# Gated-H3 forward and backward on one core: which engine transposes the gate gradient of three tiles, and how the FFT stage is ordered

## The chip, the core and the metric

The kernel runs on one core of a Trainium2 chip. A core has TensorE (PE, matrix products, whose weight loads the profile shows apart as PEld), VectorE (DVE), ScalarE (ACT), GpSimd (POOL) and SyncE (SP), and 16 DMA engines. The metric is the device time in microseconds (us) of one execution.

## The reference

What is computed is a block with a long convolution and a gated linear unit, forward and then backward by `jax.vjp`. S = 2048 positions, D = 512 channels, F = 1376 hidden columns.

```python
xn = layernorm(q)
k_shift = sum_t k_pad[:, t:t+S, :] * shift_k[:, 3-t]     # 4 taps
kv = k_shift * v
y  = irfft(rfft(kv, 2S) * rfft(ssm_k, 2S))[:, :S] + kv * ssm_D
s  = xn * y
h  = sigmoid(xn @ w_gate) * (xn @ w_up)
out = q + s * silu(h @ w_down)
# and the gradients of q, k, v, shift_k, ssm_k, ssm_D, w_gate, w_up, w_down for a given grad_out
```

The outputs are `out` and the nine gradients. The FFT is done as products with cosine and sine tables on TensorE.

## The kernel before

The program is not issued as it is written. A recorder, class Rec, takes down every operation with what it reads and writes (`add`); at the end `order()` makes one static order for each engine, and `emit()` issues it. So every instruction stands at line 522 in the profile, and the order of the code decides only between operations that the planner holds ready at the same time. `order()` simulates: each operation has an estimated duration (`cost`, `dcost`), each engine a time at which it is free, and in each step the operation that can start first is taken, of several the one that was recorded first.

- **Either engine.** An evacuation of PSUM (`evac`, line 238) may go to ScalarE or VectorE. VectorE takes it if ScalarE would come too late for it by more than 0.4 us, or 1.6 us where VectorE has other work waiting (lines 420 to 426). `op.bias` (0.3 us for PSUM of 2-byte type, which is what transposes leave there) is taken off VectorE's start in this comparison.
- **Dependent neighbours.** From operation `late` to operation `early`, an operation on VectorE or ScalarE that reads what the same engine wrote is taken as ready 0.034 us after the other's end (line 507, `r = fin + 0.034`), and an independent one may be taken in between, with a look-ahead of 0.125 us (`near`). Outside this stretch the successor counts as ready when the engine is free. Before, `late` is set at the end of the FFT stage (line 1076), `early` at the end of stage B.

The work has three stages.

**FFT stage** (operations 0 to 2405, up to about 130 us). Four streams are interleaved by `run_streams`: strG, the forward products of the gated unit (`f_gen`) for nine tiles of 128 positions in the order 15, 13, 11, 9, 7, 5, 0, 1, 2; strK, the transform of the convolution's kernel in four channel groups (`k_t` transposes the input, `step1` is the first product, `flip` transposes on TensorE, `step3` the second product); strV, shifted k times v (four taps on VectorE, each on 128x2048 elements, multiply and add, then `step1`); strX, `flip` and `step3` of kv, the products of the spectra on VectorE, and back (`inv3`, `inv1`). `gen_ci` transposes the tables. It begins with `gen_fft_consts`, which makes the tables on VectorE and ScalarE (Sin), and with the loads: `ld_KT`, `ld_k` (k and, on the same queue, its halo of three rows), `ld_v`, `ld_x`, `ld_w` (columns of both weights), all on SP's queue; skr (shift_k) and Dcol_b (ssm_D) on ScalarE's queue. `k_t(0)` adds Dcol_b to the first column before it transposes. Four products with a row of ones spread skr over the partitions (skb), which strV reads.

**Stage B** (`stepB`), tile by tile 0 to 15: `z_gen` (the down projection and the gradient of the gate, dz), `d_gen` (gradient through w_down, which needs dz transposed, dzT), `x_gen` (gradient of the input) and the rest of the `f_gen` tiles. dzT of tile 0 and of tiles 13 to 15 is made by four TensorE transposes and an evacuation, that of tiles 1 to 12 by one DMA transpose on SP's queue (line 1155).

**Last stage**: gradients of the weights (`dW`) and the backward convolution (`frontC`, `backC`).

SBUF is one tile that an arena divides (all its parts are called slab in the profile), PSUM likewise (psum).

Of the kernel before, what the change touches and what calls it, by code (L numbers as in the profile page):

```python
# [16 lines left out]
P = 128  # L17
# [6 lines left out]
NJ = 16  # L24
# [128 lines left out]
def esize(dt):  # L153
    return 4 if dt in (f32, i32) else 2


class Op:
    __slots__ = ("n", "alts", "deps", "succ", "wait", "ready", "dma", "tiles", "done", "fin", "eng", "soft", "bias")


class EngRec:
# [9 lines left out]
class Rec:  # L171
# [8 lines left out]
    def __init__(self, nc, tc, slab, psum):  # L180
        self.nc, self.tc, self.psum = nc, tc, psum
        self.slab_name = slab.name
        self.ops = []
        self.lastw, self.readers = {}, {}
        self.late, self.early = 1 << 30, 1 << 30
        self.cache = {}
        for e in self.ENGS:
            setattr(self, e, EngRec(self, e))
# [47 lines left out]
        return r  # L236

    def evac(self, dst, src, n):
        op = self.add([("scalar", "copy", (dst, src), {}), ("vector", "tensor_copy", (dst, src), {})])
        op.bias = 0.3 if esize(src.ap.dtype) == 2 else 0  # L240

    def add(self, alts):
        op = Op()
# [106 lines left out]
    def order(self):  # L350
# [55 lines left out]
        while ndone < len(ops):  # L406
            best = None
            for e in self.ENGS:
                near = 0.125 if e in ("vector", "scalar") and self.late <= lo < self.early else 0.0
                while soon[e] and soon[e][0][0] <= free[e] + near:  # L410
                    heapq.heappush(now[e], heapq.heappop(soon[e])[1])
                c = None
                if now[e]:
                    n0 = now[e][0]
                    if near and ops[n0].ready > free[e]:
                        n0 = min((n for n in now[e] if ops[n].ready <= free[e] and n < n0 + 60), default=n0)
                    c = (max(free[e], ops[n0].ready) if near else free[e], n0, e, 0)
                elif soon[e]:
                    c = (soon[e][0][0], soon[e][0][1], e, 0)
                if either and e in ("scalar", "vector"):  # L420
                    o = min(either, key=lambda o: (max(o.ready, free[e]) - (o.bias if e == "vector" else 0.0), o.n))
                    s = (max(o.ready, free[e]), o.n, e, 1)
                    late = free["scalar"] - s[0] + o.bias
                    if e == "scalar" or late > (0.4 if c is None or c[0] > s[0] + 0.6 else 1.6):
                        if c is None or s[:2] < c[:2]:
                            c = s
                if c is not None and (best is None or c[:2] < best[:2]):
                    best = c
            if best is None:
                raise RuntimeError("the order is stuck: " + str({k: len(v) for k, v in blocked.items()}))  # L430
            t, n, e, shared = best
            op = ops[n]
            if shared:
                either.remove(op)
            else:
                if now[e]:
                    now[e].remove(n)
                    heapq.heapify(now[e])
                else:
                    heapq.heappop(soon[e])  # L440
            q = 1 if shared and e == "vector" else 0
            new = [v for v in op.tiles if v.bank is None]
            if new:
                got = slot(new[0].kind)
                if got is None:
                    blocked[new[0].kind].append(op)
                    continue
                if got[0] > t:
                    op.ready = got[0]
                    push(op)  # L450
                    continue
                new[0].bank = got[1][0]
                for b in got[1]:
                    owner[b] = new[0]
            alt = op.alts[q]
            d = 0.0
            if op.dma:
                occ, d = self.dcost(alt)
                me, other = ("gpsimd", "hw") if e == "gpsimd" else ("hw", "gpsimd")
                t = max(t, pipe[me] - 12.0)  # L460
                t0 = max(pipe[me], t + 1.5)
                share = min(d, max(0.0, pipe[other] - t0))
                pipe[me] = t0 + d + share
                if share:
                    pipe[other] += share
                fin = pipe[me] + (DSL if t > 6 else 1.0)
            else:
                occ, lat = self.cost(alt)
                if e == "scalar" and alt[1] == "activation":
                    f = {ACT.Sin: "sin", ACT.Sigmoid: "sig"}.get(alt[2][2])  # L470
                    if f and f != table:
                        table = f
                        occ, lat = occ + 1.28, lat + 1.28
                fin = t + lat
            free[e] = t + occ
            op.done, op.fin, op.eng = True, fin, e
            seq.append((op, q, t, occ, d))
            ndone += 1
            while lo < len(ops) and ops[lo].done:
                lo += 1  # L480
            while held and held[0] <= lo + LOOK:
                o = ops[heapq.heappop(held)]
                o.ready = max(o.ready, t)
                push(o)
            for v in op.tiles:
                v.left -= 1
                v.last = max(v.last, fin)
                if v.left == 0:
                    for b in range(8):
                        if owner[b] is v:  # L490
                            owner[b] = None
                            banks[b] = v.last + 0.05 + PSL
                    for kind, lst in blocked.items():
                        for o in lst:
                            o.ready = max(o.ready, 0.0)
                            push(o)
                        lst.clear()
            for s in op.succ:
                if s < 0:
                    o = ops[~s]  # L500
                    o.wait -= 1
                    if o.wait == 0:
                        push(o)
                    continue
                o = ops[s]
                if e == o.alts[0][0] and len(o.alts) == 1 and not op.dma:
                    r = fin + 0.034 if e in ("vector", "scalar") and self.late <= o.n < self.early else t + occ
                else:
                    r = fin + 0.045 + (PSL if o.alts[0][0] == "tensor" and not op.dma else 0.0)
                o.ready = max(o.ready, r)  # L510
                o.wait -= 1
                if o.wait == 0:
                    push(o)
# [123 lines left out]
def kernel_impl(ctx, tc, A_q, A_k, A_v, A_shift_k, A_ssm_k, A_ssm_D, B_x, B_w_gate, B_w_up, B_w_down,  # L637
# [23 lines left out]
    def ps_acc(shape, dt=f32, name=None):  # L661
        return nc.ps("acc", shape, dt)
# [151 lines left out]
    def ld_v(cp):  # L814
        vg = vg_r.next()
        nc.sync.dma_start(vg, vC[:, :, cp * GW:(cp + 1) * GW])
        stA["vg", cp] = vg
# [4 lines left out]
    def ld_x(i):  # L822
        T[i]["xq"] = xq_r.next()
        nc.sync.dma_start(T[i]["xq"], qC[:, i, :])
    nc.scalar.dma_start(skr, A_shift_k.rearrange("(o d) t -> o (d t)", o=1))
    nc.scalar.dma_start(Dcol_b, A_ssm_D.rearrange("(cg p) -> p cg", p=P))
    ld_KT(0)
    ld_x(SEQ[0])
    ld_x(SEQ[1])
# [1 line left out]
    def ld_w(f0, f1):  # L831
        for w, src in ((wg, B_w_gate), (wu, B_w_up)):
            nc.sync.dma_start(w[:, :, f0:f1], src[:, f0:f1].rearrange("(db p) f -> p db f", p=P))
    ld_w(0, 512)
    ld_k(0)
    ld_v(0)
    ld_x(SEQ[2])
    ld_w(512, 1024)
    ld_w(1024, F)
# [22 lines left out]
        pass  # L862
    next(consts)
    f_ln(SEQ[0])
    next(consts)
    f_xt(SEQ[0])
    f_ln(SEQ[1])
    next(consts)
    for db in range(4):
        pb = ps_acc([512])  # L870
        nc.tensor.matmul(pb[:], ones1, skr[:, db * 512:(db + 1) * 512], start=True, stop=True)
        nc.scalar.copy(skb[:, :, db * 128:(db + 1) * 128], pb[:].rearrange("p (d t) -> p t d", t=4))
    ld_KT(1)
    ld_k(1)
    ld_v(1)
# [197 lines left out]
    for r in (KT_r, KC_r, kh_r, vg_r, acc_r, term_r, kvt_r, QgK_r, QgV_r, QfK_r, QfV_r, KF_r, Ks_r, Bg_r, Xc_r, P1_r, Ci_r):  # L1073
        r.free()
    PS["mm"], PS["wide"] = "mm1", False
    nc.late = len(nc.ops)


    zw = {k: Ring(ar, [D], at=kv_off["kh"] + 1024 * q) for q, k in enumerate(("sigz", "gate", "s_out", "dgate", "t2"))}
# [53 lines left out]
    def z_gen(i):  # L1133
# [18 lines left out]
        nc.vector.tensor_tensor(t2, t2, sigz, ALU.add)  # L1152
        nc.vector.tensor_tensor(dzA[:, i, :], dgate, t2, ALU.mult)
        T[i]["dzT"] = dzT_r.next()
        if 0 < i < NJ - 3:
            nc.sync.dma_start_transpose(T[i]["dzT"], dzA[:, i, :])
        else:
            pt = ps_tr([4, 128], name="ps_dzT")
            for db in range(4):
                nc.tensor.transpose(pt[:, db, :], dzA[:, i, db * 128:(db + 1) * 128], ident)  # L1160
            nc.evac(T[i]["dzT"], pt[:], 512)
# [380 lines left out]
```

## Time and profile before

| what | us |
|---|---|
| median of 13 runs | 519.66 (518.68 to 521.81) |
| the profiled execution | 519.77 |
| its span, first to last instruction | 518.0 |
| busy: TensorE | 491.9 |
| busy: VectorE | 390.5 |
| busy: ScalarE | 351.2 |
| busy: GpSimd | 126.0 |

The page cuts the span in 40 slices, and a digit gives the busy share of an engine in a slice in tenths. A matmul's record runs from its issue to its modelled end, so TensorE's busy time holds waits within a group of products too. The timeline puts successive instructions of one form into one row: start, duration, engine, line, operation, output and input, and how many. In the groups by shape a row gives count, summed busy time, the mean of one in ns and, behind the next bar, the idle time of the engine just before them with what ended it.

The first slices of ScalarE and VectorE:

```profile
DVE  8789998777848789867779988427658678873754
ACT  7799999889975564465545546426879968776621
```

### The profile page before, as it was taken

Reading aid. Unit: us, or ns where it says so; the run is one execution under the profiler, and the core shown is the slowest. Engines: PE = TensorE matmul, PEld = TensorE weight load, DVE = VectorE, ACT = ScalarE, POOL = GpSimd, SP = SyncE. Lnnn points to the kernel's source line nnn. Section 1 sums busy time; section 2 is a strip of 40 time slices with the busy share of each in tenths; the row PEclk is TensorE's granted clock in tenths of the full one; section 3 lists DMA queues with packets and bytes.
Section 4 is the critical chain, followed back from the end, with each engine's and each line's share of the span. In section 5 each row is a group of like instructions: output and inputs, shape, how many; then the busy total and the mean of one; then the engine's idle time right before and its main releaser. Section 6 shows DMA issues by size and latency. Waiting matters only on the chain.

```text
span 518.0 us, 13489 instructions
## 1 busy us (share of the span) xinstructions
PE 491.9 (95%) x5381; PEld 352.7 (68%) x5437; DVE 390.5 (75%) x771; ACT 351.2 (68%) x468; POOL 126.0 (24%) x243
## 2 busy tenths in 40 slices
PE   4899898999999999999999999999999999999997
PEld 3788697898987676666666556644676756775744
DVE  8789998777848789867779988427658678873754
ACT  7799999889975564465545546426879968776621
POOL 7344423455503423414153311000000000000000
PEclk9999998999999999999999999999999999999999
DMA  8999985688999555737399947898798689999984
GB/s 221 295 279 330 296 260 183 208 253 245 235 198 236 156 160 149 221 100 200 117 251 232 267 156 179 208 295 215 180 254 227 189 260 215 259 199 253 200 219 120
DMA packets 181705, 112.93 MB, mean 218 GB/s; under 512 B 131433, under 2 KB 166153, under 8 KB 181386
## 3 DMA queue, kind: packets, MB, share of 16 engines
q1 hardware_dynamic: 170008, 78.17, 62.9%
q0 software_dynamic: 11104, 33.89, 19.9%
q8 instruction: 42, 0.69, 0.5%
q14 instruction: 21, 0.17, 0.1%
q10 hardware_dynamic: 530, 0.01, 0.1%
HBM read 37.65 MB, written 45.72 MB: 161 GB/s over the span
## 4 chain that ended last, share of the span: by engine, by line
PE 74%; ACT 10%; DVE 7%; issue 3%; DMA 3%; POOL 1%; SPq 0%; ACTq 0%; DVEq 0%; POOLq 0%
PE psum L522 74%; ACT slab L522 10%; DVE slab L522 7%; DMA out_dram<-slab 1%; DMA slab<-in_A_ssm_D_dram 1%; POOL slab L522 1%; DMA slab<-in_grad_out_dram 0%; SPq L522 0%; ACTq L522 0%; POOL hF_d L522 0%; POOL out_dram L522 0%; DVEq L522 0%; POOLq L522 0%
## 5 line engine op out<-in xcount | busy, mean ns | idle before, releaser
L522 PE MATMUL psum<-slab 128*128 128x128 bf16 (+5 forms) x5381 | 491.9, 254 | 22.4 <-ACT slab L522 10.3
L522 PEld LDWEIGHTS <-slab 128*128 128x128 bf16 (+2 forms) x5437 | 352.7, 99 | 161.3 <-issue 17.0
L522 DVE TENSOR_TENSOR slab<-slab 128x512 bf16<-128x512 bf16 (+6 forms) x488 | 268.6, 601 | 51.8 <-ACT slab L522 34.2
L522 ACT CAST slab<-psum 128x1024 bf16<-128x1024 f32 (+5 forms) x272 | 219.7, 848 | 93.4 <-PE psum L522 79.7
L522 ACT ACTIVATE slab<-psum 128x512 bf16<-128x512 f32 (+2 forms) x80 | 54.2, 680 | 39.3 <-PE psum L522 36.1
L522 ACT ACTIVATE slab<-slab 128x512 bf16<-128x512 bf16 (+3 forms) x71 | 56.8, 810 | 15.0 <-DVE slab L522 14.1
L522 ACT COPY slab<-psum 128x1024 bf16<-128x1024 bf16 (+1 forms) x43 | 38.4, 939 | 14.1 <-PE psum L522 13.9
L522 POOL DMA_DIRECT2D out_dram<-slab x32 | 17.4, 545 | 95.8 <-DVE slab L522 95.8
L522 DVE TENSOR_TENSOR slab<-psum,slab 128x512 bf16<-128x512 f32 (+2 forms) x47 | 29.3, 627 | 14.1 <-ACT slab L522 12.2
L522 DVE CAST slab<-psum 128x1024 bf16<-128x1024 f32 (+2 forms) x22 | 24.6, 1117 | 15.0 <-PE psum L522 12.9
L522 POOL MEMSET slab<- 1x384 bf16 (+2 forms) x13 | 4.8, 375 | 116.7 <-PE psum L522 116.3
L522 POOL DMA_DIRECT2D hF_d<-slab x48 | 26.0, 544 | 23.3 <-DVE slab L522 22.3
L522 DVE SCALAR_TENSOR_TENSOR slab<-psum,slab 128x512 bf16<-128x512 f32 x16 | 11.0, 690 | 27.1 <-PE psum L522 27.1
L522 POOL DMA_DIRECT2D KK_d<-slab x32 | 17.4, 545 | 27.6 <-ACT slab L522 20.5
L522 POOL DMA_DIRECT2D slab<-in_A_q_dram x29 | 16.0, 554 | 15.3 <-DVE slab L522 4.7
L522 DVE SCALAR_TENSOR_TENSOR slab<-slab 128x512 bf16<-128x512 bf16 (+3 forms) x41 | 17.1, 417 | 0.9
L522 DVE STREAM_TRANSPOSE slab<-slab 128x1024 f32<-128x1024 f32 x8 | 14.3, 1824 | 2.7 <-ACT slab L522 2.7
L522 DVE TENSOR_SCALAR slab<-slab 128x1 f32<-128x1 f32 (+9 forms) x48 | 12.1, 268 | 4.6 <-POOL slab L522 3.7
L522 POOL TENSOR_TENSOR slab<-slab 128x1 f32<-128x1 f32 x16 | 11.2, 700 | 17.5 <-DVE slab L522 17.2
L522 POOL DMA_DIRECT2D slab<-hF_d x18 | 9.7, 541 | 12.7 <-PE psum L522 11.5
L522 DVE BATCH_NORM_STATS2 slab<-slab 128x6 f32<-128x512 bf16 x16 | 10.9, 686 | 0.0
L522 DVE COPY slab<-psum 128x1024 bf16<-128x1024 bf16 (+1 forms) x14 | 9.0, 649 | 2.3 <-ACT slab L522 1.7
(20 smaller groups left out, 36.2 us busy)
## 6 DMA issues: line engine op xcount, KB each, us to landing
KK_d<-slab POOLq DMA_DIRECT2D x32, 256.0 KB, 5.0
slab<-KK_d SPq DMA_DIRECT2D x16, 512.0 KB, 4.5
slab<-in_A_k_dram SPq DMA_DIRECT2D x8, 512.0 KB, 7.8
hF_d<-slab POOLq DMA_DIRECT2D x32, 128.0 KB, 4.6
slab<-slab SPq DMA_DIRECT2D x32, 128.0 KB, 5.2
out_dram<-slab POOLq DMA_DIRECT2D x32, 128.0 KB, 2.9
uF_d<-slab SPq DMA_DIRECT2D x32, 128.0 KB, 2.5
gF_d<-slab SPq DMA_DIRECT2D x32, 128.0 KB, 2.9
```

Source lines behind the costliest of these rows:

```text
L522: getattr(getattr(self.nc, eng), meth)(*[place(v) for v in a], **{x: place(v) for x, v in k.items()})
```

## The change

Four things change together.

1. `evac` sets no bias, and `order()` does not use one.
2. `late` is 0 from the start and not set again, so the rule for dependent neighbours holds in the FFT stage too.
3. The start: Dcol_b is loaded ahead of skr; k and v of group 0 are loaded ahead of the first columns of the weights; the four skb products and their copies are recorded right behind the first layernorm.
4. dzT of tiles 10, 11 and 12 is made by TensorE transposes and an evacuation instead of a DMA transpose.

```diff
-        self.late, self.early = 1 << 30, 1 << 30
+        self.late, self.early = 0, 1 << 30
...
     def evac(self, dst, src, n):
-        op = self.add([("scalar", "copy", (dst, src), {}), ("vector", "tensor_copy", (dst, src), {})])
-        op.bias = 0.3 if esize(src.ap.dtype) == 2 else 0
+        self.add([("scalar", "copy", (dst, src), {}), ("vector", "tensor_copy", (dst, src), {})])
...
-                    o = min(either, key=lambda o: (max(o.ready, free[e]) - (o.bias if e == "vector" else 0.0), o.n))
+                    o = min(either, key=lambda o: (max(o.ready, free[e]), o.n))
                     s = (max(o.ready, free[e]), o.n, e, 1)
-                    late = free["scalar"] - s[0] + o.bias
+                    late = free["scalar"] - s[0]
...
+    nc.scalar.dma_start(Dcol_b, A_ssm_D.rearrange("(cg p) -> p cg", p=P))
     nc.scalar.dma_start(skr, A_shift_k.rearrange("(o d) t -> o (d t)", o=1))
-    nc.scalar.dma_start(Dcol_b, A_ssm_D.rearrange("(cg p) -> p cg", p=P))
...
-    ld_w(0, 512)
     ld_k(0)
     ld_v(0)
+    ld_w(0, 512)
...
     f_ln(SEQ[0])
+    for db in range(4):
+        pb = ps_acc([512])
+        nc.tensor.matmul(pb[:], ones1, skr[:, db * 512:(db + 1) * 512], start=True, stop=True)
+        nc.scalar.copy(skb[:, :, db * 128:(db + 1) * 128], pb[:].rearrange("p (d t) -> p t d", t=4))
     next(consts)
     f_xt(SEQ[0])
     f_ln(SEQ[1])
     next(consts)
-    for db in range(4):
-        pb = ps_acc([512])
-        nc.tensor.matmul(pb[:], ones1, skr[:, db * 512:(db + 1) * 512], start=True, stop=True)
-        nc.scalar.copy(skb[:, :, db * 128:(db + 1) * 128], pb[:].rearrange("p (d t) -> p t d", t=4))
...
-    nc.late = len(nc.ops)
...
-        if 0 < i < NJ - 3:
+        if 0 < i < 10:
             nc.sync.dma_start_transpose(T[i]["dzT"], dzA[:, i, :])
         else:
             pt = ps_tr([4, 128], name="ps_dzT")
             for db in range(4):
                 nc.tensor.transpose(pt[:, db, :], dzA[:, i, db * 128:(db + 1) * 128], ident)
             nc.evac(T[i]["dzT"], pt[:], 512)
```

From about 30% of the program on, the new order of every engine is the old one but for the three tiles of point 4. Before that, 28 evacuations change their engine and many operations their place.

More of the change, by code (lines that the diff above doesn't have):

```diff
@@ L157 @@
 class Op:
-    __slots__ = ("n", "alts", "deps", "succ", "wait", "ready", "dma", "tiles", "done", "fin", "eng", "soft", "bias")
+    __slots__ = ("n", "alts", "deps", "succ", "wait", "ready", "dma", "tiles", "done", "fin", "eng", "soft")
 class EngRec:
```

## Prediction

> **What bounds the kernel now.** The profiled execution has a span of 518.0 us in a time of 519.77; the median of the thirteen runs shown is 519.66, so sums on the trace are read against 519.77 and 0.11 is taken off at the end. About ±1.04 us (0.2%) is what can be told from no change.
>
> I read the page's engine rows first, then its slices, then the windows of the stages.
>
> ```profile
> PE 491.9 (95%) x5381; PEld 352.7 (68%) x5437; DVE 390.5 (75%) x771; ACT 351.2 (68%) x468; POOL 126.0 (24%) x243
> ...
> PE   4899898999999999999999999999999999999997
> ...
> PEclk9999998999999999999999999999999999999999
> ```
>
> TensorE is busy 95% at full clock, but a matmul that waits for its buffer counts as busy too. So I price a step by its pitch in a stream:
>
> ```profile
> 34.70 0.61 PE L522 MATMUL psum<-slab 128*128 128x128 bf16 x8 [0.35 <-ACT slab L522]
> 35.62 0.55 PE L522 MATMUL psum<-slab 128*128 128x128 bf16 x7 [0.31 <-ACT slab L522]
> ```
>
> Eight 128-column steps took 0.61 us. One alone takes 0.22 (their mean in the groups by shape), so one more costs (0.61 - 0.22)/7 = 0.056 us; the second row is transposes against the identity (gen_ci): (0.55 - 0.22)/6 = 0.055, the same. A 512-column step, from 21 in 4.70 us that begin at 275.66, is (4.70 - 0.38)/20 = 0.216.
>
> With these, 20 to 70 us holds 648 x 0.056 + 19 x 0.216 = 40 us of TensorE work in 50; 260 to 300 holds 39.4 in 40. Summed the same way over the span, TensorE loses 28 us before 100 us (14 of them in the first 20, some 9 from 20 to 70, 5 from 80 to 98), nothing worth naming from 100 to 360, and 3 after. **A TensorE instruction added after 100 us costs its full pitch; before 100 us the time is set by who feeds TensorE.** That is read in the windows (time, and busy time of each engine with its instructions, then clock, DMA share, GB/s):
>
> ```profile
> 20.00:70.00 50.00, 44.12 (x667) 39.17 (x670) 45.17 (x61) 46.58 (x58) 21.47 (x40) 1.00 0.99 298
> ...
> 80.00:98.00 18.00, 15.54 (x199) 13.29 (x199) 16.11 (x23) 16.55 (x19) 7.64 (x13) 0.91 0.48 155
> ...
> 104.00:130.00 26.00, 25.57 (x410) 23.71 (x412) 19.29 (x34) 23.52 (x29) 14.41 (x27) 1.00 0.85 249
> ```
>
> From 20 to 70 us VectorE (45.2) and ScalarE (46.6) are both nearly full; from 30 on each is busy over 39 of 40. At 104 to 130 TensorE is full and ScalarE has 26 - 23.5 = 2.5 us to spare.
>
> **Part 1: dzT of tiles 10, 11, 12 on TensorE.** Three DMA transposes leave SP's queue, three evacuations of 128x512 and twelve TensorE steps come. In the trace the transpose of tile 10 was issued at 274.25, landed at 278.62, and d_gen(10) began at 280.2; tiles 11 and 12 took 4.3 and 4.8 us and no product waited for them. So nothing is won by removing them, and the stores behind them on SP gain about 1.2 us of issue each, which nothing waits for. The evacuations (0.60 us each) go to ScalarE, busy 20.8 of the 40 us from 260 to 300; other TensorE work stands between. If that cover failed, d_gen would wait at most one evacuation per tile, 1.8 us in all.
>
> The price of the steps is where a rule speaks against the change. The row: 12 x 0.056 = **+0.67 us**. The Trainium skill ("TensorE: Matmul & The Clock Gate", Part 4, PE-mode transpose) gives about 275 ns for a 128x128 transpose inside a kernel and says that transposes don't count as busy for the clock: by it, an estimate of 12 x 0.275 = 3.3 us. The transposes in this trace run at 0.055 behind each other with the clock at 1.00, so I take the row; 3.3 is the upper end.
>
> **Part 2: no lean by type.** Before, an evacuation of 2-byte PSUM leaned to VectorE by 0.3 us. The new static order has seven more bf16 evacuations of 1024 on ScalarE, and four fewer f32 ones there.
>
> ```profile
> L522 ACT CAST slab<-psum 128x1024 bf16<-128x1024 f32 x150 | 148.8, 1042 | 28.9 <-PE psum L522 19.1 <-DVE slab L522 5.5 <-DMA out_dram<-slab 2.7
> L522 ACT COPY slab<-psum 128x1024 bf16<-128x1024 bf16 x32 | 32.3, 1055 | 4.8 <-PE psum L522 4.6
> ...
> L522 DVE CAST slab<-psum 128x1024 bf16<-128x1024 f32 x18 | 22.0, 1221 | 8.7 <-PE psum L522 6.6 <-DMA out_dram<-slab 2.1
> L522 DVE COPY slab<-psum 128x1024 bf16<-128x1024 bf16 x12 | 8.2, 686 | 1.0 <-PE psum L522 0.6 <-ACT slab L522 0.5
> ```
>
> ScalarE: 7 x 1.06 - 4 x 1.04 = +3.2 us; VectorE: 4 x 1.22 - 7 x 0.69 = +0.1. VectorE takes a bf16 tile 0.37 us cheaper than ScalarE and an f32 tile 0.18 dearer, so the exchange costs work on the pair. By place, from the two orders with these means: up to about 98 us ScalarE has +1.1 and VectorE +0.4; from there to 130 ScalarE gets another 2.8 us.
>
> **Part 3: the order of the FFT stage with the delay of dependent operations.** VectorE has 52 of 201 neighbouring pairs there in which the second reads the first; after, 31 of 197. In the trace a dependent successor starts 0.03 us after the end (84.63 after 84.60), an independent one about 0.08 before it (80.04 in the operation of 79.43 to 80.12): 21 x 0.11 = 2.3 us of VectorE. Of this the sum takes the row; "VectorE: DVE Perf Modes" (The DRAIN you can't avoid) lets no successor start before the pipe is empty, by which reordering would give 0. The same section says that one not held starts earlier, so the row stands.
>
> At 80 to 98 us TensorE starves; the chain of waits goes through VectorE there:
>
> ```profile
> 81.26 3.34 DVE slab L522 x4
> ```
>
> In the timeline VectorE runs five 128x2048 products of strV (1.22 us each, depending on each other) from 80.64 on, with one f_gen product between them, and the product of strX that TensorE needs starts only at 87.03. In the new order one strV product and one small operation fewer stand ahead of it: 1.22 + 0.55 = 1.8 us. ScalarE's queue stands full beside it until 90, so I count the share of VectorE on this chain: (3.34 + 0.69)/18 x 1.8 = -0.4.
>
> **Part 4: the start.** D's load is issued first (0.75 instead of 1.30): it landed at 6.26 and VectorE waited 0.53 for it, so VectorE is up to 0.56 earlier. The four skb broadcasts and their copies move before later Sin operations, same work. k and v of group 0 go ahead of the first 1 MB of weights. SP needed 3.17 to 9.53 us to issue k's two pieces; w_up landed at 9.91, and behind k and v would land near 16, while the first f_gen product began at 14.75. So f_gen(15) is up to 1.5 us later, but k's second halo gets off the queue earlier, and strV(0), which waited until 28.92 for a halo issued at 23.96, starts about 3 us sooner and fills VectorE's 4.2 idle us of 20 to 30.
>
> **Sum.** Up to 104 us: VectorE -2.3 + 0.4 = -1.9, ScalarE +1.1. Both are full and hand work to each other, so half of the sum, -0.4; the stall -0.4; the start I put at 0 (ScalarE's queue reaches the same point at 30 us with one more evacuation done, but the first f_gen later). Together **-0.8**, bounds -2.9 (VectorE alone decides: -2.3 - 0.56 + 0.38 - 0.4) and +1.5 (the weights decide). 104 to 130: +2.8 us on ScalarE against 2.5 spare: 0.4 if all the idle time can be used, 2.8 if none; TensorE needs its buffers in turn, so the middle, **+1.4** after taking 0.2 off for the 1 us that VectorE gives back. Part 1 **+0.7**. In all +1.3: 521.0 in its own execution, 520.9 against the median. Own range: -0.8 + 0.4 + 0.7 = +0.3 at the low end; at the high end the FFT stage loses a third of its upper bound, +0.5, and ScalarE's extra counts whole: +0.5 + 2.8 + 0.7 = +4.0. So 519.9 to 523.7.
>
> **Rivals.**
> A, faster: VectorE is what TensorE waits for all through the FFT stage, so its dependent gaps and the stall at 81 to 88 come off in full: -2.9 + 0.4 + 0.7 = -1.8, **517.9**; with the whole 1.8 of the stall and ScalarE's extra hidden, -3.6, 516.1. For: the chain at 81 us, DVE 39.4 of 40 from 30 to 70. Against: ScalarE 39.6 of 40 there. It decides once strX's product ends more than ScalarE's backlog ahead of 87.
> B, no net change: FFT stage -0.8, ScalarE's extra at 104 hidden, twelve steps +0.7: **519.6**. For: VectorE has 6.7 idle us there. Against: the order is fixed, so idle VectorE takes nothing over.
> C, slower at the start: the weights landing at 16 hold the first f_gen and with it ScalarE's sigmoid: +1.5 instead of -0.8, **523.2**. For: DMA 0.96 busy in the first 20 us. Against: step1 products are there to be done.
>
> **Chances.** Forecast 0.36, A 0.34, B 0.18, C 0.12. Faster takes A and a little of B, 0.35; within 0.2% B and the lower edge of the forecast, 0.20; slower 0.45. The range reaches into A to 516.8 and into C to 523.5.
>
> **What would show it.** Part 1: no idle TensorE at 270 to 300, twelve more steps, clock 1.00. Part 2: ScalarE near 26 of 26 at 104 to 130 and TensorE waiting on it; if TensorE streams there, the +1.4 falls. Part 3: strX's product earlier than 87.03 against f_gen(7), TensorE's loss of 80 to 98 below 5 us; if it is under 3, A holds. Part 4: strV(0) before 27, first f_gen near 16. Wrong altogether if the first 20 us move by over 2 us either way.

## The result, and the profile after

The changed kernel took 524.85 us (median of 11 runs, 522.46 to 527.71), the kernel before 519.59 in the same comparison (48 runs): a ratio of 1.0097, 95% interval 1.0082 to 1.0113. It is slower, as forecast, but by four times as much as the forecast of 520.9 said, and above both upper ends that the prediction names (523.5 and 523.7). The profiled execution took 523.54 us, with a span of 521.6.

One sentence of the description ahead of the prediction was wrong and has to be put right first: it is not from about 30% of the program on that the new order is the old one, but only in about the last 30%. Stage B is reordered too, up to its last tiles, and there the time went.

The page's engine rows and slices, after:

```profile
PE 492.0 (94%) x5392; PEld 351.4 (67%) x5449; DVE 390.9 (75%) x769; ACT 354.2 (68%) x473; POOL 125.7 (24%) x243
...
PE   5888898999999999999999799999999999998996
...
PEclk9999999999999999999999999999999999999999
```

There is a new hole: the 7 in slice 23 of TensorE's row, from 287 to 300 us, where the row of before has a nine. The windows of the stages, after:

```profile
20.00:70.00 50.00, 45.22 (x691) 40.48 (x695) 45.95 (x59) 48.93 (x60) 23.34 (x41) 1.00 1.01 301
...
80.00:98.00 18.00, 16.00 (x248) 14.41 (x249) 16.38 (x23) 17.03 (x21) 7.07 (x13) 1.00 0.68 210
...
104.00:130.00 26.00, 25.57 (x408) 23.65 (x410) 17.72 (x29) 23.91 (x30) 13.56 (x27) 1.00 0.89 243
```

The FFT stage became faster: from 80 to 98 us 248 TensorE records instead of 199 and a clock of 1.00 instead of 0.91. With the two pitches of the prediction (0.056 and 0.216 us a step), the work that TensorE lost up to 130 us fell from 28.6 to 24.8 us. (Some traces lack matmul records; counting a 512-column step for each weight load without one gives these sums to about half a us.) In the three other executions with each order of the FFT stage (e1, e4 and e8 below have the old one, e2, e3 and e9 the new one) it is about 28 and about 25, so 3 to 4 us are won. The clock is not what won them: e1 and e4 have the old order and a clock of 1.00 from 80 to 98 us, and lose 27.9 and 28.1. From 104 to 130 us TensorE is as full as before. The groups by shape show the exchange of types:

```profile
L521 ACT COPY slab<-psum 128x1024 bf16<-128x1024 bf16 x39 | 41.0, 1100 | 1.6 <-PE psum L521 1.6
...
L521 DVE COPY slab<-psum 128x1024 bf16<-128x1024 bf16 x5 | 3.4, 685 | 1.1 <-PE psum L521 1.1
```

Later they are lost again. By 290 us the loss is 25.3, by 310 it is 30.5, where before it stays at 28.7. The windows of that time (the granted clock is the third number from the end):

```profile
295.00:300.00 5.00, 1.91 (x6) 0.74 (x7) 3.35 (x9) 1.66 (x2) 1.08 (x2) 0.88 1.13 249
300.00:305.00 5.00, 5.00 (x46) 3.23 (x45) 4.36 (x13) 1.61 (x4) 1.08 (x2) 0.78 0.69 224
```

TensorE is idle for 3.59 us, from 294.50 to 298.09, and right behind that the granted clock is below 1.00: 0.12 and 0.22 of 5 us each are 1.7 us more. Together this is the 5.2 us. What led to the idle time, the chain of waits from 280 to 310 us says (start, duration, what):

```profile
283.38 13.14 DMA slab<-in_grad_out_dram
...
298.09 7.67 PE psum L521 x61
```

A load of 128 KB of grad_out, that of tile 13, took 13.14 us; its kind takes 4.2 on the median of the page before. VectorE waits for it, and TensorE for VectorE's dz. The timeline of SP's queue beside it, then that of GpSimd's:

```profile
282.23 4.61 SPq L521 DMA_TRANSPOSE slab<-hF_d  x1
...
288.54 9.89 SPq L521 DMA_TRANSPOSE slab<-hF_d  x1
```

```profile
281.26 1.60 POOL L521 DMA_DIRECT2D hF_d<-slab  x3 [2.27 <-DVE slab L521]
...
282.85 0.54 POOL L521 DMA_DIRECT2D slab<-sF_d  x1
283.38 0.54 POOL L521 DMA_DIRECT2D slab<-in_grad_out_dram  x1
```

The two rows of SP are the last two of four transposing loads of h for the weight gradients (`ld_L`, 0.5 MB each), whose place in SP's order has changed. The first stands in the middle of a burst that GpSimd issues from 281.3 to 286.5, the second behind it, while it is still in flight. The burst is three stores of h of tile 14, a load of 352 KB of sig of tile 13, and loads and a store of 128 KB. The windows of 5 us, first after, then before (the last two columns are the busy share of the DMA engines and GB/s):

```profile
285.00:290.00 5.00, 4.95 (x54) 3.54 (x54) 4.37 (x14) 2.06 (x4) 1.19 (x4) 1.00 1.22 103
290.00:295.00 5.00, 4.50 (x32) 2.24 (x29) 0.79 (x3) 2.89 (x5) 0.00 (x0) 1.00 1.06 111
```

```profile
285.00:290.00 5.00, 5.00 (x25) 2.27 (x24) 4.97 (x14) 1.23 (x2) 2.55 (x8) 1.00 1.04 259
290.00:295.00 5.00, 4.95 (x58) 3.81 (x58) 4.21 (x14) 3.61 (x6) 1.54 (x3) 1.00 1.15 280
```

The DMA engines are as busy and move less than half. That is the theory to test, **J**: the transposing loads and GpSimd's burst slow each other, and the new order has made them meet. A meeting alone is not enough: the kernel before has a transposing load among GpSimd's transfers too (279.99 to 284.57), and it did no harm. The rival, **Z**: the three tiles on TensorE are what costs, by waits for dz. In the tables and expectations "loss" is TensorE's lost work as summed above, in slices of 10 us; the expectations name a slice by its start, so that their "120 us" is up to 130 here, and their "150" up to 160.

### The profile page after: what moved, and what is told of

It is laid out like the page before. It is cut to its first block, busy times and chain, and to the rows that moved or that the text cites. A ratio compares the mean times of both kernels' runs of the same rounds, so it can differ in the third digit from the quotient of the medians.

```text
span 521.6 us, 13526 instructions
## 1 busy us (share of the span) xinstructions
PE 492.0 (94%) x5392; PEld 351.4 (67%) x5449; DVE 390.9 (75%) x769; ACT 354.2 (68%) x473; POOL 125.7 (24%) x243
## 4 chain that ended last, share of the span: by engine, by line
PE 68%; ACT 15%; DVE 6%; issue 4%; DMA 4%; POOL 2%; SPq 0%; ACTq 0%; DVEq 0%; POOLq 0%
PE psum L521 68%; ACT slab L521 15%; DVE slab L521 6%; DMA slab<-in_grad_out_dram 3%; POOL slab L521 1%; DMA out_dram<-slab 1%; SPq L521 0%; ACT L521 0%; POOL hF_d L521 0%; ACTq L521 0%; DVEq L521 0%; POOLq L521 0%; POOLq L1524 0%
## 5 line engine op out<-in xcount | busy, mean ns | idle before, releaser
L521 PE MATMUL psum<-slab 128*128 128x128 bf16 (+4 forms) x5392 | 492.0, 254 | 25.4 <-ACT slab L521 12.1
L521 PEld LDWEIGHTS <-slab 128*128 128x128 bf16 (+1 forms) x5449 | 351.4, 99 | 165.6 <-issue 18.4
L521 ACT CAST slab<-psum 128x1024 bf16<-128x1024 f32 (+5 forms) x267 | 216.7, 859 | 86.1 <-PE psum L521 66.7
L521 ACT ACTIVATE slab<-psum 128x512 bf16<-128x512 f32 (+2 forms) x80 | 55.3, 692 | 34.7 <-PE psum L521 34.2
L521 ACT COPY slab<-psum 128x1024 bf16<-128x1024 bf16 (+1 forms) x53 | 48.8, 969 | 19.6 <-PE psum L521 19.6
L521 DVE CAST slab<-psum 128x1024 bf16<-128x1024 f32 (+3 forms) x27 | 30.0, 1111 | 16.9 <-PE psum L521 14.9
L521 POOL DMA_DIRECT2D slab<-in_grad_out_dram x16 | 8.6, 540 | 7.2 <-DMA out_dram<-slab 6.0
```

What stands on the lines that cost most here:

```text
L521: getattr(getattr(self.nc, eng), meth)(*[place(v) for v in a], **{x: place(v) for x, v in k.items()})
```

## The experiments

### The loads moved apart, and together

Two runs take part 1 alone and the change without it; two move nothing but transposing loads on SP. A small helper takes an operation out of the finished order and puts it behind another one.

e1, the kernel before with part 1 alone:

```diff
-        if 0 < i < NJ - 3:
+        if 0 < i < 10:
```

> The kernel before with part 1 alone: dzT of tiles 10 to 12 on TensorE. Planner, start and types as before. Theory J (the profile after lost 5 us at 293 to 298 because the transposing loads of h for the weight gradients ran in the DMA engines at the same time as GpSimd's loads, an accident of the new order): here two of these loads stand behind each other on SP, earlier than in the kernel after, so no 5 us stall is forced; +0.7 us for twelve steps, 519.5 to 521. Theory Z (the three tiles on TensorE are themselves what costs, by waits for dz and the evacuation): 523 to 525, with TensorE idle around tiles 10 to 12.

e2, the kernel after with that line as it was before:

> The kernel after with dzT of tiles 10 to 12 by DMA as before; bias, late and the start as after. The FFT stage is the one of the kernel after, which ended 3.9 us earlier than before. Theory J: the stall goes only if the new order separates the transposing loads from GpSimd's loads: then 515 to 516.5; if they still meet, 520 to 524 with a load of over 10 us. Theory Z: 515 to 516.5 whatever the loads do.

e3, the kernel after with two transposing loads put later:

```diff
         seq = self.order()
+        def put(n, m):
+            s = seq.pop([r[0].n for r in seq].index(n))
+            seq.insert([r[0].n for r in seq].index(m) + 1, s)
+        put(4539, 4632)
+        put(4541, 4539)
```

> The kernel after, with nothing changed but SP's order: the two last transposing loads of h (of four) are issued behind the stores of tile 11 instead of among those of tile 10. Theory J: GpSimd's loads of tile 13 land in 4 to 5 us instead of 13, TensorE has no gap at 294 to 298, time 516 to 519.5. Theory Z: unchanged, 523 to 525.

e4, the kernel before with one put earlier (`put(4531, 4239)`):

> The kernel before, with nothing changed but SP's order: one transposing load of h is issued some 2.5 us earlier, behind the first stores of tile 9, so that it runs together with GpSimd's loads and stores of 276 to 280. Theory J: these take 8 to 13 us instead of 4 to 5, and tile 12 starts late: 521 to 525. Theory Z: no change, 519 to 520.

| run | us | ratio to before (519.82) |
|---|---|---|
| e1 | 527.14 (525.97 to 527.70) | 1.0131 (1.0105 to 1.0156) |
| e2 | 516.77 (516.11 to 517.22) | 0.9932 (0.9906 to 0.9959) |
| e3 | 517.53 (517.17 to 518.57) | 0.9954 (0.9932 to 0.9975) |
| e4 | 521.57 (518.41 to 529.36) | 1.0034 (1.0014 to 1.0055) |

**e3 settles what cost the time in the changed kernel.** Two transposing loads in other places of SP's order take 7.3 us off it (524.85 to 517.53), and it is then faster than the kernel before. Its windows of the same time:

```profile
285.00:290.00 5.00, 5.00 (x52) 3.44 (x50) 4.39 (x14) 1.66 (x3) 1.58 (x5) 1.00 0.86 220
290.00:295.00 5.00, 5.00 (x37) 2.76 (x36) 4.05 (x12) 4.48 (x7) 1.08 (x2) 1.00 0.52 165
```

TensorE is full, and the loads of grad_out from 275 to 300 us take 4.8 us on the median. e4 is the opposite: the same work, one load put into a burst, and the runs spread over 11 us (3.4 for the kernel before). Its profiled execution was a mild one (519.83 us), in which the grad_out load of tile 12 took 8.5 us instead of 5.0.

e2 does not separate the theories, since both allowed 515 to 516.5. But it limits J, which said 520 to 524 if loads and burst still meet. The same burst runs there with a transposing load in it, issued later than in the changed kernel and behind the burst's loads:

```profile
280.77 1.61 POOL L521 DMA_DIRECT2D hF_d<-slab  x3 [1.93 <-DVE slab L521]
...
283.93 5.81 SPq L521 DMA_TRANSPOSE slab<-hF_d  x1
```

The load of grad_out took 6.3 us instead of 13.1, and TensorE did not wait. So not every meeting is slow; more on this at e13.

e3 less e2 is an estimate of what the twelve transposes on TensorE cost: 0.76 us against 0.67 forecast. It is not a clean one, because the orders of the two differ in stage B from about 260 us on.

e1 lies above the ranges of both theories, and went wrong by another way than J as it was put: none of GpSimd's loads is slow as in the changed kernel (that of grad_out at 280.72 took 5.5 us). TensorE waits at 319.61 for the dz of tile 14 (timeline rows of TensorE and of ScalarE's sigmoid of that tile):

```profile
319.61 2.58 PE L522 MATMUL psum<-slab 128*128 128x128 bf16 x23 [2.94 <-DVE slab L522]
```

```profile
314.92 0.60 ACT L522 ACTIVATE slab<-psum 128x512 bf16<-128x512 f32 x1 [6.26 <-PE psum L522]
```

From the sigmoid to dz it takes 4.6 us, with the epilogue of another tile between on both engines. The order of e1 has TensorE work of 1.8 us between the last product of z and the transposes of tile 14, and of 2.7 us for tile 13; the orders before and after have about 5 (sums of the pitches over the steps between). e8 tests this.

### More cover for e1's transposes

e8, e1 with the transposes of tiles 13 and 14 and their evacuations put behind more products:

```diff
+        for ns, m in ((range(4682, 4687), 4797), (range(4809, 4814), 4886)):
+            for n in ns:
+                put(n, m)
+                m = n
```

> The kernel with part 1 alone (527.1 us), and in it the dz transposes of tiles 13 and 14 with their evacuations issued later on TensorE and ScalarE, behind six products of 512 columns more each: TensorE then has about 4.7 and 5 us of other work between the last product of z and its transposes, as before, instead of 2.7 and 1.8. Theory O (part 1 alone lost its time because the new order left too little work ahead of these transposes): 520.5 to 524, no gap of TensorE at 319. Theory J (contention of the loads): 526 to 528, unchanged.

It took 523.85 us (523.44 to 524.29), 3.3 less than e1, and the wait before the transposes of tile 14 is gone. But only part of the 3.3 is shown to come from it. In the profiled executions TensorE lost 4.9 us from 290 to 320 in e1 and some 3.5 in e8, where a product of x_gen of tile 13 now waits 1.6 us for VectorE's work on that tile, and over 1 us is lost at 304 as in e1. The other 2 us e1 had lost at 165, where x_gen of the first tile waited for transposed weights that landed late (166.75, in e8 161.22). That cannot come from e1's order, which is that of the kernel before up to about 270 us; why the load was late is not shown. So Z holds for e1 in part: a wait for dz was there and cover removed it. Of the 7.3 us of e1, 4.1 are left in e8, some 0.7 of them the twelve steps; the rest is not settled.

### The other parts alone

e5 has part 4 alone (the start), e6 part 3 alone (the rule for dependent operations), e7 part 2 alone:

```diff
-        op.bias = 0.3 if esize(src.ap.dtype) == 2 else 0
+        op.bias = 0
```

> The kernel before with the new start alone (part 4). The kernel after without part 1 gained 3.05 us (516.77 against 519.82), nearly all before 104 us. Theory S (VectorE starts strV sooner and fills its idle time of 20 to 30 us): 517.3 to 518.5, the loss of TensorE up to 104 us 26 to 27 instead of 28. Theory P (the order by dependent operations brings the gain): 519.5 to 520, loss 28. Theory W of the prediction's rival C (the later weights decide): 521.

> The kernel before with the rule for dependent operations in the FFT stage alone (part 3). Theory P: 517 to 518.3, TensorE loses under 4 us from 80 to 98 and the span of the FFT stage shrinks by 1.5 to 2.5 us. Theory S: 519.3 to 520.

> The kernel before without the lean by type alone (part 2). The prediction's own step (more work for ScalarE at 104 to 130): 520.5 to 521.5. Rival (ScalarE's queue hides it): 519.3 to 520.2.

e11 has parts 3 and 4, e14 parts 2 and 3:

> The kernel before with parts 3 and 4 (dependent operations, start), types and tiles as before. The FFT stage's gain is a sum of parts (0.8 for the start and 1.6 to 2.2 for the order, from the loss of TensorE in the two single runs): 516.8 to 518, loss at 150 us about 26. If the parts do not add: 518.5 to 519.5.

> The kernel before with parts 2 and 3 (types, dependent operations), start and tiles as before. If types only cost and the order only gains: 518.5 to 520. If the two gain together (the loss of TensorE at 120 us was 24.6 with all parts, 26.4 with the order alone, 27.7 with the types alone): 516.5 to 518.5, loss at 120 us about 25.5.

| run | parts | us | ratio to before | loss up to 130, up to 360 us |
|---|---|---|---|---|
| before | none | 519.59 | 1 | 28.6, 28.6 |
| e5 | start | 520.02 | 1.0007 (0.9997 to 1.0017) | 27.6, 27.9 |
| e6 | order | 518.79 | 0.9984 (0.9967 to 1.0001) | 26.4, 27.7 |
| e7 | types | 534.30 | 1.0296 (1.0254 to 1.0338) | 27.7, 42.6 |
| e11 | order, start | 523.78 | 1.0067 (1.0042 to 1.0091) | 27.1, 33.8 |
| e14 | order, types | 521.78 | 1.0035 (1.0021 to 1.0049) | 31.7, 33.8 |
| e2 | all but the tiles | 516.77 | 0.9932 (0.9906 to 0.9959) | 24.6, 25.8 |

The last column is from one profiled execution each, with a scatter of about 0.7 us (28.6, 28.1 and 27.9 in three executions whose FFT stage has the same order). The ratios are to the kernel before in the same comparison as the run (519.72 for e5 to e7, 520.04 for e11, 519.82 for e14 and e2). In the loss of the FFT stage all three together win 4.0 us, the order alone 2.2. The 1.0 and 0.9 of the start and of the types are hardly more than the scatter; no cost of the types is seen there, but order and types together (e14) lose 31.7, where the order alone loses 26.4. The times don't follow. e5 is at the edge of what theory P allowed, e6 between its two theories, and e7, e11 and e14 are slower than any theory said, each with a late transfer on its chain. In e7 it is J again, 20 us earlier. A row of the chain, then one of SP's queue:

```profile
269.24 14.93 DMA slab<-in_grad_out_dram
```

```profile
272.84 12.63 SPq L522 DMA_TRANSPOSE slab<-hF_d  x1
```

The second row holds SP for 12.6 us, and the DMA transpose of dz of tile 10 stands behind it. TensorE is idle for 11.95 us until that tile's dzT has landed. In e11 the chain goes through a copy of K's spectrum behind the transposing loads of w_down, in e14 through a store beside the plain load of w_down (1.25 MB):

```profile
137.94 9.10 DMA slab<-slab
```

```profile
107.40 9.96 DMA KK_d<-slab
```

No run moved these two transfers, so that their company made them late is not shown. In e14 that company is no transposing load.

e9 and e10 move loads again: in the kernel after only one of the two (`put(4539, 4632)`), and in e7 three of them, to about where the kernel before has them.

```diff
+        put(4531, 4210)
+        put(4532, 4277)
+        put(4533, 4361)
```

> The kernel after (524.85 us), with only one transposing load moved on SP: the third of the four, issued at 282.2 in the middle of GpSimd's burst, goes behind the stores of tile 11; the fourth keeps its place behind the stores of tile 10. Theory J: with nothing transposing while the burst of 281 to 284 runs, the loads land in 4 to 6 us: 517 to 519.5. Rival (two transposing loads close together are what fills the DMA engines, whatever GpSimd does): the two now stand close behind each other again, 521 to 525.

> The kernel with part 2 alone (534.3 us), with three transposing loads moved back on SP to about the places they have in the kernel before (behind the transpose of tile 10, behind the stores of tile 9, behind the transpose of tile 11). Theory J (all of its 14.6 us came from the loads meeting, and the types themselves cost nothing): 519 to 521. Theory of the prediction's step (ScalarE's extra work costs 1.4): 521 to 522. If the loads were not the cause: over 528.

e9 took 519.05 us (516.63 to 522.58; ratio 0.9981, 0.9962 to 1.0000): most of the 7.3 us are gone with one load, as J said, but the runs spread. e10 took 521.74 us (520.03 to 525.14; 1.0035, 1.0018 to 1.0052): of the 14.6 us of part 2 alone 12.6 went with the places of the loads. The 1.7 that are left against its own comparison (520.04) lie above what J expected and in the range of the prediction's step on ScalarE. In its profiled execution (520.86 us) TensorE lost 28.8 us up to 360, as before (28.6), so they are not shown to belong to the types.

### The transfers by themselves

e12 and e13 compute nothing and only move the same kinds of data, in phases:

```python
def turned():     # two transposing loads of 0.5 MB on SP
    for q in range(2):
        nc.sync.dma_start_transpose(L0[:, 16 * q:16 * q + 16, :], hF_d[0][q].rearrange("p j f -> p (j f)"))
def burst():      # three stores, 352 KB of sF_d, three loads of 128 KB, a store, on GpSimd
    ...
```

> Leaves out the whole computation; outputs are zeros. It only moves data, in phases with a barrier between: two transposing loads of 0.5 MB on SP alone; GpSimd's burst of eight transfers (three stores of 128 KB, a load of 352 KB, three loads of 128 KB, a store) alone; both together; the burst beside two plain loads of 0.5 MB on SP; both together again. Theory J: transposing alone about 10 us, burst alone about 7, together 20 us or more, that is over the sum of the two, with a packet of either kind three times as long or more; beside plain loads no longer than the sum. Rival (the engines only share their time): together no longer than the sum, some 15 us.

> Leaves out the whole computation; outputs are zeros. Phases with a full barrier between, on the same data: two transposing loads alone; GpSimd's burst alone; both; both beside a stream of TensorE products, of VectorE products, of ScalarE activations; transposing loads beside all three engines; the burst beside all three; both beside all three; both again. Theory C (the engines' use of SBUF slows the transposing loads and what shares the DMA engines with them): both beside one of the streams takes 18 us or more against 11 to 12.5 without. Rival (what the engines do makes no difference): 11 to 12.5 in all phases with both, and what slows them in the kernel stays open.

In e12 the barriers let the loads of SP start a phase too early, so that the transposing loads were never alone. Beside the burst the two took 12.4, 11.2 and 12.1 us from the first issue to the last landing; J had expected 20 or more, and that missed. The burst took 8.9 us beside plain loads and 7.1 alone. e13 has full barriers. Its windows, one for each phase: transposing alone, burst alone, both, both beside VectorE, both beside all three engines, both again with no engine at work:

```profile
17.60:24.40 6.80, 0.00 (x0) 0.00 (x0) 0.00 (x0) 0.00 (x0) 0.65 (x11) 1.00 0.70 154
24.80:32.10 7.30, 0.00 (x0) 0.00 (x0) 0.00 (x0) 0.00 (x0) 4.33 (x9) 1.00 0.53 176
32.70:44.20 11.50, 0.00 (x0) 0.00 (x0) 0.00 (x0) 0.00 (x0) 4.47 (x13) 1.00 0.94 202
60.00:70.70 10.70, 0.00 (x0) 0.00 (x0) 9.91 (x24) 0.00 (x0) 4.39 (x12) 0.59 0.93 213
118.20:135.00 16.80, 13.07 (x59) 5.80 (x60) 12.77 (x30) 10.08 (x16) 4.53 (x13) 0.96 0.89 140
135.60:151.30 15.70, 0.00 (x0) 0.00 (x0) 0.00 (x0) 0.00 (x0) 4.51 (x13) 0.50 0.85 148
```

Alone the two take 6.7 and 7.1 us, 13.8 in sum. Together, from the first issue to the last landing, the same transfers took 12.0 us with no engine at work, 14.1 beside TensorE, 11.4 beside VectorE, 14.4 beside ScalarE, 16.7 beside all three, and 15.7 with no engine at work again. So theory C falls: what the engines do in SBUF is not needed for a slow meeting. The same two sets of transfers take from less than to 1.2 times their sum, at a busy share of 0.85 to 0.94 and 140 to 213 GB/s.

One thing separates quick and slow meetings in the nine that e12 and e13 hold: when SP issues the second transposing load, counted from the burst's first store.

| meetings | second transposing load after | both done after |
|---|---|---|
| e12 | 2.3, 3.1, 3.1 us | 12.4, 11.2, 12.1 us |
| e13, quick | 2.3, 2.3 us | 12.0, 11.4 us |
| e13, slow | 1.2, 1.4, 1.1, 1.9 us | 14.1, 14.4, 16.7, 15.7 us |

In the slow ones it is issued ahead of the burst's first load of 128 KB, in the quick ones behind it. The changed kernel fits (1.0 us, ahead of the loads, 13.1 us for that of grad_out), and so do e2 and e9 (3.2 and 3.5 us, behind them, 6.3 and 5.8 us). e1 does not: a transposing load at 276.50 stands ahead of the loads there, and none is slow. No run varied this alone, so it is a lead and not a shown cause.

The trace's packets show what a slow meeting looks like. Alone, a 256-byte packet of a transposing load takes 18 ns, and a 4 KB packet of the burst 192 on the mean. In the slow stretches of the last two phases (124 to 132 and 141 to 149 us) the means are 40 and 33 ns for the first kind and 870 and 600 for the second; in the changed kernel, from 286 to 292 us, 55 ns, and 1,240 for the six large packets that start there. Most small packets still take 18 ns (73 to 85%), and some over 100. Why, stays open.

## Why the prediction was wrong

- **Part 1 failed, in the step on SP's queue.** The prediction said that nothing is won by removing the three DMA transposes and that the stores behind them on SP gain some issue time, "which nothing waits for", and priced the part at +0.67. Added to the other three parts it cost 8.1 us (524.85 against 516.77 in e2). The price of the steps was about right: some 0.76 by e3 and e2, so the row of the trace, not the 3.3 us that came from the page on TensorE. What was left out is the rest of SP's queue. With the transposes gone and stage B reordered, two transposing loads of h came to stand in GpSimd's burst, and where they stood cost 7.3 us (e3): something does wait, VectorE for the load of grad_out and TensorE for VectorE. That the same line added to the kernel before costs 7.3 us too (e1) looks like a coincidence: there it is in part a wait for dz, and the rest is open. The prediction's own sign for this part, no idle TensorE from 270 to 300 us, failed with the 3.59 us of the hole. The description's wrong sentence hid all this: no step of the sum looked at the order of stage B.
- **The FFT stage: right in kind, too small.** Forecast -0.8, with -2.9 as the bound if VectorE alone decides. e2, which has all parts but the tiles, is 3.05 us faster than before: the bound, and a little more. The prediction's reason against it, a full ScalarE, gave way: from 20 to 70 us it had 3.4 us to spare and used 2.4 of them (48.93 busy after 46.58). The product of strX that TensorE needs starts at 83.62 instead of 87.03, 3.4 us earlier where 1.8 were forecast. TensorE's loss from 80 to 98 fell from 5.2 to 2.5 us, under the 3 that the prediction named as the sign of rival A. So A was right on this stage in its sign and its size. That VectorE alone decided is not shown: the order alone (e6) brings 0.9 us, not clear of noise, and in the new kernel the chain at 80 to 94 us goes through ScalarE:

```profile
82.32 3.63 ACT slab L521 x5
...
89.92 2.83 ACT slab L521 x4
```

- **104 to 130 us: +1.4 fell.** ScalarE is busy 23.91 of 26 there (23.52 before), and TensorE lost 0.6 us from 104 to 130, against 0.5 before. Forecast were 2.8 us more of ScalarE; 0.4 came. Most of its extra work stands at 20 to 70 us, where it had time.
- **The start** was right in its steps: the weights' second piece landed at 16.03 as estimated, the sigmoid of tile 15 began at 19.13 instead of 18.65, strV(0) at 24.44 instead of 28.92. Its gain was put at 0; e5 shows 1.0 us less loss up to 130 us, hardly more than the scatter, and no gain in the time.
- **The sum, and luck.** All but part 1 was forecast at +0.6 (-0.8 and +1.4) and measured at -3.05; part 1 was forecast at +0.67 and measured at +8.1. The two errors have opposite signs. That the kernel came out slower, as forecast, is luck: the term that was to make most of the slowdown, ScalarE at 104 to 130 us, did not come, and one that was not in the sum did.
- **Slips.** 2.8 us of extra work against 2.5 spare leave 0.3, not 0.4, which does not move the +1.4. Two ranges stand in the prediction, 519.9 to 523.7 and 516.8 to 523.5; the result is above both.

The fastest version of all is e2, the change without its first part: 516.77 us.

## What to carry to other kernels

Where one planner orders the whole program, no edit is local: list where each DMA queue's order has changed in later stages before pricing it at its own place, large transfers first. Look for large transposing loads in a burst on another queue that something waits for soon, above all ahead of the burst's loads: not every such meeting is slow, but here the loads of 13.1 and 14.9 us instead of 4 stood in one. Before a change is dropped or kept, run it once with the suspicious transfer moved by hand: here that turned a loss of 1% into a gain of 0.5%. And try the parts of a change one by one and together: the times of the parts did not add up.

## What the hardware showed that was not expected

A transposing load and plain transfers in flight together can cost more than one after the other: up to 16.7 us against 13.8 in e13, with packets two to six times as long on the mean, and in the kernels a 128 KB load took 13.1 and 14.9 us instead of 4.2. The Trainium skill ("DMA: Bandwidth & Descriptors", Rules for kernel authors) says that a transpose next to ordinary DMAs needs nothing. That is meant of correct data, and no run here speaks against it; of time it does not hold in these runs. Reading the DMA engines' busy share would not have warned: it was 1.22 in the slow window and 1.04 in the quick one, with 103 and 259 GB/s moved.
